# A gated attention-and-MLP decode kernel: the first weight load, 512 rows of wq, issued as two halves of 64 partitions from two engines

## The chip, the cores and the metric

The kernel runs on one core of one Trainium2 chip. The metric is the device time of one execution in microseconds; the time before is the median of three runs.

## The reference

One decode step for eight sequences: attention over a cached K and V, an MLP behind a layer norm, and a gate that mixes the two. Everything is bf16.

```python
# x: [8, 1, 576]; 32 heads of 128; 4096 cached keys; MLP width 4608
g = sigmoid((x * gate_w).sum(-1, keepdims=True))
q = (x @ wq) -> [8, 32, 1, 128]                    # wq: [576, 4096]
p = softmax(q . k_cache * 128 ** -0.5)             # k_cache: [8, 32, 4096, 128]
a = (p . v_cache) -> [8, 1, 4096] @ wo             # wo: [4096, 576]
b = gelu(layernorm(x) @ w1 + b1) @ w2 + b2         # w1: [576, 4608], w2: [4608, 576]
out = g * a + (1 - g) * b
```

The K and V caches are 268 MB each, the weights together about 20 MB. Each byte of them is read once.

## The kernel before

**Groups.** A group `n` (32 of them) is one sequence and eight heads. Its K is 8.4 MB, laid out in SBUF as 128 partitions with 256 keys each, and so is its V. The scores are made by VectorE: `mult` (L501) multiplies 32 keys of each partition with the group's query `q_n`, TensorE adds up pieces of the products (L512 and L183), and VectorE reduces the rest (L524). Eight such steps make the scores of a group. After the softmax TensorE multiplies with V (L565), while VectorE is on the next group's K.

**Buffers and order of the loads.** `KR` holds one and a half K groups, `VB` one V group. SyncE's queue carries nearly every transfer, in program order, with a wait ahead of some of them. K of group n+1 (`load_k`, L333) waits until VectorE has read the half of the buffer that it overwrites; V (`load_v`, L344) waits until TensorE has finished with the V before it.

**The start.** Before the first group the same buffers hold weights. SyncE issues, in this order: rows 0 to 511 of wq into `VB` (4 MB: 128 partitions of 32 KB, four rows each), the last 64 rows of wq (`halves`, 128 partitions of 4 KB), K of group 0 in two parts, w1 in two parts. The second of these waits for `c_yps`, the last of three ScalarE blanks that write zeros into PSUM banks. Then comes w2 (`load_w2`), which waits for the last Q matmul (`p_Q`), because it goes into `VB` too; then K of group 1, which waits for the last product of group 0; then V of group 0, a first part that waits for `p_Q`, and a second that waits for the MLP's last matmul (L654), which reads w2 out of that place.

ScalarE's queue carries the small loads: x (8 partitions), gate_w, b1, b2, all issued right behind the three blanks in ScalarE's program. Its other work at the start is the table loads, the blanks (L289), two constants from the identity, the square root and the sigmoid (L410, L411), and copies.

x is needed for the layer norm and the gate (VectorE, from L398; gate_w at L408), for the transposes of x and of its normed form on TensorE (L425), and so for Q (L452): 40 matmuls with wq as the moving operand. TensorE runs in program order: transposes of x, of the normed x, then Q. ScalarE copies Q out (L455), TensorE spreads it to the partitions (L466), ScalarE makes `q_n` of it (L476), and the first product of group 0 follows on VectorE.

`op(engine, fn, waits, dma)` records an instruction for an engine with what it waits for; `load` is the same for a DMA with a semaphore of its own, so that the DMAs all carry line L296. The order in which the operations are recorded is the program order of each engine.

Of the kernel before, what the change touches and what calls it, by code (L numbers as in the profile page):

```python
# [41 lines left out]
class Stream:  # L42
# [11 lines left out]
    def op(self, engine, fn, waits=(), dma=None, side=0):  # L54

        rec = [fn, [w for w in waits if w is not None], None, dma, (engine, side)]
        self.ops[engine].append(rec)
        if dma is not None:
            return ("dma", *dma)
        return ("op", engine, rec)  # L60
# [84 lines left out]
def bass_gated_mix__mha_block_cached__mixer_channel_mlp__decode_kernel(  # L145
# [18 lines left out]
    op = S.op  # L164
# [4 lines left out]
    def pstride(t):  # L169
        return t[tuple([slice(None)] * len(t.shape))].ap[0][0]  # L170

    def view(t, offset, shape):
        ap = []
        stride = 1
        for n in reversed(shape[1:]):
            ap.insert(0, [stride, n])
            stride *= n
        return bass.AP(tensor=t, offset=offset, ap=[[pstride(t), shape[0]]] + ap)
# [16 lines left out]
    wq_sb = view(VB, 0, [128, 4, SK])  # L195
    wq_t = view(VB, 4 * SK, [128, SK // 2])
# [86 lines left out]
    sV = nc.alloc_semaphore("sV")  # L283
    nK, nV = [0], [0]

    zeros = bass.AP(tensor=mA, offset=1, ap=[[pstride(mA), 128], [0, 512]])

    def blank(ps):
        return aside("scalar", lambda e: e.activation(out=ps[:, :], in_=zeros, func=ACT.Copy), [c_mA])  # L289
# [1 line left out]
    c_mA = op("gpsimd", lambda e: e.memset(mA[:], 0.0))  # L291
    c_ps = [blank(ps) for ps in tr_ps]
    c_yps = blank(y_ps)

    def load(engine, dst, src, name, waits=()):
        return op(engine, lambda e: e.dma_start(dst, src), waits, dma=(nc.alloc_semaphore(name), 16))  # L296


    x_flat = A_x.rearrange("b s d -> (b s) d")
    out_flat = out.rearrange("b s d -> (b s) d")  # L300
# [5 lines left out]
    def halves(w):  # L306

        return w[512:576, :].rearrange("r (s n) -> (r s) n", s=2)

    ld_wq = [load("sync", wq_sb, A_wq[0:512, :].rearrange("(p kt) n -> p kt n", kt=4), "ld_wqa"),  # L310
             load("sync", wq_t, halves(A_wq), "ld_wqb", [c_yps])]


    def kv_src(cache, n):
# [21 lines left out]
    def load_k_half(n, s):  # L336
        dst = view(KR, k_base(n) + s * THIRD, [128, NTK, DH])
        k_land[n, s] = load("sync", dst, kv_src(A_k_cache, n)[:, s * NTK:(s + 1) * NTK, :], f"sKh{n}_{s}")
# [561 lines left out]
```

## Time and profile before

| | |
|---|---|
| median of 3 runs | 1295.03 us (1294.98 to 1295.03) |
| span of the profiled execution | 1293.2 us |
| the profiled execution's own time | not given apart from the span |
| bytes moved, mean rate | 557.07 MB, 431 GB/s |
| busy: TensorE, VectorE, ScalarE, GpSimd | 57%, 66%, 6%, 1% |
| DMA engines, SyncE's queue / ScalarE's queue | 11520 packets, 556.93 MB / 200 packets, 0.03 MB |

The profile gives one execution: busy times by engine, 40 equal slices of the span, the DMA queues, the chain of work that ended last, groups of instructions by line, and the DMA issues. "SPq" and "ACTq" are the sequencers of SyncE and ScalarE, which issue DMAs; q1 is SyncE's DMA queue and q10 is ScalarE's. A timeline row has start, duration, engine, line, operation, the tiles written and read, how many instructions it merges, and in brackets the idle time ahead of it with what ended it.

### The profile page before, as it was taken

What the parts mean: (1) busy time and instruction counts of PE and PEld (TensorE: products, weight loads), DVE (VectorE), ACT (ScalarE), POOL (GpSimd) and SP (SyncE); (2) the same over time, 40 slices, a digit from 0 to 9 for tenths busy, and PEclk for the clock granted to TensorE, in tenths of its full rate; (3) what the DMA queues carried; (4) which work ended last, traced back from release to release, by engine and by line L of the source; (5) the groups of instructions that cost most, each with busy time, mean ns of one, the idle gap of its engine ahead of it and who ended that gap; (6) DMA issues with size and microseconds to landing.
All of it is one profiled execution on the core that took longest, in us unless ns stands there. A gap on an engine that the chain in (4) does not pass through costs nothing.

```text
span 1293.2 us, 10904 instructions
## 1 busy us (share of the span) xinstructions
PE 733.4 (57%) x4824; PEld 142.9 (11%) x3032; DVE 852.0 (66%) x1078; ACT 73.2 (6%) x164; POOL 12.7 (1%) x23
## 2 busy tenths in 40 slices
PE   3755566455556555556555556555556555557556
PEld 0211111011111011111011111001111001111003
DVE  3646667766667766667766667766668766667763
ACT  3300000000000000000000000000000000000001
POOL 0100000000000000000000000000000000000001
PEclk8978888877898787799778889777888877898888
DMA  9999999999999999999999999999999999999998
GB/s 406 426 447 424 430 442 428 434 436 432 442 426 430 444 426 430 442 430 434 436 430 442 426 430 444 426 430 442 430 434 436 430 442 428 428 444 428 432 434 356
DMA packets 11728, 557.07 MB, mean 431 GB/s; under 512 B 1448, under 2 KB 1608, under 8 KB 2120
## 3 DMA queue, kind: packets, MB, share of 16 engines
q1 hardware_dynamic: 11520, 556.93, 99.7%
q8 instruction: 5, 0.08, 0.0%
q10 hardware_dynamic: 200, 0.03, 0.0%
q14 instruction: 3, 0.02, 0.0%
HBM read 556.95 MB, written 0.01 MB: 431 GB/s over the span
## 4 chain that ended last, share of the span: by engine, by line
DMA 67%; DVE 18%; PE 9%; issue 5%; DVEq 1%; ACT 0%; SPq 0%; ACTq 0%
DMA KR<-in_A_k_cache_dram 65%; DVE p L501 15%; PE psb L183 7%; DVE s_sb L524 2%; DMA KR<-in_A_wo_dram 2%; PE psb L512 2%; DVEq L524 0%; DVEq L137 0%; SPq L296 0%; ACT psb L289 0%; PE psb L755 0%; ACT L289 0%; ACTq L296 0%; DVE p L851 0%; ACT sel_f L391 0%
## 5 line engine op out<-in xcount | busy, mean ns | idle before, releaser
L501 DVE TENSOR_TENSOR p<-KR,q_n 128x4096 bf16<-128x4096 bf16 x256 | 581.9, 2284 | 212.7 <-DMA KR<-in_A_k_cache_dram 212.7
L183 PE MATMUL psb<-p,ident 128*128 128x512 bf16 x1792 | 485.8, 416 | 0.0
L512 PE MATMUL psb<-p,ident 128*128 128x512 bf16 x256 | 112.3, 439 | 509.6 <-DVE p L501 509.6
L524 DVE TENSOR_REDUCE s_sb<-psb 128x512 f32 (+1 forms) x256 | 175.6, 686 | 107.5 <-PE psb L183 61.0
L512 PEld LDWEIGHTS psb<-p,ident 128*128 128x128 bf16 x256 | 26.1, 102 | 964.3 <-DVE p L501 963.9
L565 PE MATMUL psb<-VB,P 128*32 128x512 bf16 x1984 | 112.8, 380 | 0.0
L553 DVE TENSOR_SCALAR P<-E,own 128x256 bf16<-128x256 bf16 x256 | 53.1, 282 | 87.4 <-ACT E L550 87.4
L476 ACT ACTIVATE q_n<-q_bc 128x128 bf16<-128x128 bf16 x32 | 9.9, 310 | 871.4 <-DVE p L501 871.3
L565 PEld LDWEIGHTS psb<-VB,P 128*32 128x32 bf16 x1984 | 50.2, 97 | 47.8
L582 PE MATMUL psb<-selO,O_sb 128*128 128x8 f32 x256 | 33.9, 259 | 22.5 <-ACT O_sb L577 22.5
L582 PEld LDWEIGHTS psb<-selO,O_sb 128*128 128x128 f32 x256 | 31.0, 191 | 38.3 <-ACT O_sb L577 38.3
L577 ACT ACTIVATE O_sb<-psb 128x512 f32<-128x512 f32 x32 | 19.1, 597 | 197.9 <-PE psb L565 197.9
L572 PEld LDWEIGHTS psb<-rs,ones 128*128 128x128 f32 x64 | 12.1, 190 | 46.6 <-issue 44.4
L692 POOL TENSOR_TENSOR p<-OT_sb,fine 128x512 bf16<-128x512 bf16 (+1 forms) x4 | 5.0, 1276 | 1196.9 <-PE psb L572 1193.1
L550 ACT ACTIVATE E<-s_sb,mD 128x256 bf16<-128x256 f32 x32 | 16.0, 499 | 0.0
L541 DVE TENSOR_REDUCE mA<-s_sb 128x1 f32<-128x256 f32 x32 | 13.5, 420 | 1.1
L481 ACT ACTIVATE OT_sb<-O_n,G 128x8 bf16<-128x8 f32 x31 | 9.3, 301 | 84.3 <-DVE O_n L588 84.3
L556 DVE TENSOR_REDUCE es<-E 128x1 f32<-128x256 bf16 x32 | 13.2, 412 | 0.0
L572 PE MATMUL psb<-rs,ones 128*128 128x8 f32 x64 | 9.2, 216 | 1.3 <-DVE O_n L588 1.3
L654 PE MATMUL psb<-VB,hT_sb 128*8 128x288 bf16 x72 | 6.5, 357 | 4.7 <-POOL hT_sb L633 4.7
L557 DVE TENSOR_SCALAR rs<-own,es 128x8 f32<-128x8 f32 x32 | 7.4, 231 | 1.1
L549 DVE STREAM_TRANSPOSE mD<-mC 128x32 f32<-128x32 f32 x32 | 6.8, 212 | 1.1
(98 smaller groups left out, 125.6 us busy)
## 6 DMA issues: line engine op xcount, KB each, us to landing
KR<-in_A_k_cache_dram SPq DMA_DIRECT2D x2, 4096.0 KB, 24.8
VB<-in_A_v_cache_dram SPq DMA_DIRECT2D x1, 5376.0 KB, 27.1
VB<-in_B_w_dram SPq DMA_DIRECT2D x1, 5184.0 KB, 40.7
KR<-in_B_w_dram SPq DMA_DIRECT2D x1, 4608.0 KB, 41.2
VB<-in_A_wq_dram SPq DMA_DIRECT2D x1, 4096.0 KB, 12.5
KR<-in_A_v_cache_dram SPq DMA_DIRECT2D x1, 4096.0 KB, 22.3
VB<-in_A_v_cache_dram SPq DMA_DIRECT2D x1, 2816.0 KB, 38.4
KR<-in_A_wo_dram SPq DMA_DIRECT2D x1, 2304.0 KB, 20.7
```

The costliest lines, as they stand in the source:

```text
L183: return e.add_instruction(mybir.InstMatmult(name=nc.get_next_instruction_name(), engine=mybir.EngineType.PE, ins=[e.lower_ap(rhs), e.lowe ...
L501: v_mult[n, c] = op("vector", lambda e: e.tensor_tensor(out=p1[:, par, :, :], in0=k_of(), in1=qb, op=ALU.mult), [k_land[n, s], a_q[n], p_s ...
L512: fn = lambda e, r=r: e.matmul(tr_ps[par][:, :], lhsT=ident[:, :], rhs=r, start=True, stop=False)
L524: v_red[n, c] = op("vector", lambda e: e.tensor_reduce(out=s_of(), in_=tr_ps[par][:, :].rearrange("p (t c) -> p t c", c=CH), axis=AX.X, op ...
L541: t = op("vector", lambda e: e.tensor_reduce(out=mA[:, 0:1], in_=s_sb[:, :], axis=AX.X, op=ALU.max), [v_red[n, NC - 1], c_mA])
L550: a_exp[n] = op("scalar", lambda e: e.activation(out=E[:, :], in_=s_sb[:, :], func=ACT.Exp, bias=mD[:, 0:1], scale=1.0), [v_nm[n], v_P.get ...
L553: v_P[n] = op("vector", lambda e, h=h: e.tensor_scalar(out=P[:, :, h, :], in0=E[:, :].rearrange("p (q t) -> p q t", t=TQ), scalar1=own[:, ...
L556: t = op("vector", lambda e: e.tensor_reduce(out=es[:, :], in_=E[:, :], axis=AX.X, op=ALU.add), [a_exp[n]])
L565: p_pv[n] = op("tensor", lambda e, o=o, tq=tq, at=at, v=v: e.matmul(o, lhsT=P[:, tq, :, :].rearrange("p h t -> p (h t)"), rhs=v.rearrange( ...
L572: p_z[n] = op("tensor", lambda e: e.matmul(oz_ps[:, HB:2 * HB], lhsT=ones[:, :], rhs=rs[:, :], start=True, stop=True), [v_rs[n], v_norm.ge ...
L577: a_ev[n] = op("scalar", lambda e: e.activation(out=O_sb[:].rearrange("p t d -> p (t d)"), in_=o_ps[n // last][:, :], func=ACT.Copy), [p_p ...
L582: p_oz[n] = op("tensor", lambda e, tt=tt: e.matmul(o, lhsT=O_sb[:, tt, :], rhs=selO[:, tt, :], start=(tt == 0), stop=(tt == TQ - 1 and stop)),
```

## The change

The 4 MB load of wq's rows 0 to 511 becomes two loads of 2 MB: partitions 0 to 63 from SyncE, partitions 64 to 127 from ScalarE. Each has a semaphore of its own. Both are recorded ahead of everything else, so that ScalarE's half is the first instruction of its program, ahead of the blanks and the small loads. The first Q matmul waits for three loads of wq instead of two. The rest of the order stays.

```diff
+    def load(engine, dst, src, name, waits=()):
+        return op(engine, lambda e: e.dma_start(dst, src), waits, dma=(nc.alloc_semaphore(name), 16))
+
+    wq_src = A_wq[0:512, :].rearrange("(p kt) n -> p kt n", kt=4)
+    ld_wq = [load(e, wq_sb[p:p + 64], wq_src[p:p + 64], f"ld_wqa{p}") for e, p in (("sync", 0), ("scalar", 64))]
+
     zeros = bass.AP(tensor=mA, offset=1, ap=[[pstride(mA), 128], [0, 512]])
...
-    def load(engine, dst, src, name, waits=()):
-        return op(engine, lambda e: e.dma_start(dst, src), waits, dma=(nc.alloc_semaphore(name), 16))
-
-
...
-    ld_wq = [load("sync", wq_sb, A_wq[0:512, :].rearrange("(p kt) n -> p kt n", kt=4), "ld_wqa"),
-             load("sync", wq_t, halves(A_wq), "ld_wqb", [c_yps])]
+    ld_wq.append(load("sync", wq_t, halves(A_wq), "ld_wqb", [c_yps]))
```

## The prediction

> **What bounds the kernel now.** I read the page's head first: the span, the slices of DMA, the queues, the chain.
>
> ```profile
> span 1293.2 us, 10904 instructions
> ...
> DMA  9999999999999999999999999999999999999998
> ...
> q1 hardware_dynamic: 11520, 556.93, 99.7%
> ...
> DMA 67%; DVE 18%; PE 9%; issue 5%; DVEq 1%; ACT 0%; SPq 0%; ACTq 0%
> ```
>
> The 16 DMA engines are busy in all 40 slices, and SyncE's queue (q1) fills 99.7% of their time. The chain names DVE for 18%, but only because a K load's landing lets DVE free the buffer of the next one; the engines meanwhile work on V. The same by stages (columns after the engines: clock, DMA share, GB/s):
>
> ```profile
> 0.00:1.75 1.75, 0.00 (x0) 0.00 (x0) 0.18 (x1) 1.00 (x1) 0.98 (x9) 1.00 0.00 0
> 1.75:32.33 30.58, 11.16 (x70) 2.92 (x58) 10.76 (x20) 9.06 (x19) 0.96 (x5) 0.89 1.03 430
> 32.33:1265.83 1233.50, 703.70 (x4428) 128.01 (x2648) 833.37 (x1035) 59.62 (x138) 4.97 (x6) 0.84 1.00 433
> 1265.83:1293.20 27.37, 18.52 (x329) 12.02 (x327) 7.65 (x24) 3.47 (x7) 5.80 (x5) 0.77 0.84 349
> ```
>
> Nothing moves for 1.75 us, then the stream runs at 430 to 433 GB/s until the tail. So the time is start plus bytes over rate plus tail, and a microsecond lost or won in the first transfer reaches the end whole, unless the stream has a hole elsewhere. The median, 1295.03 us, lies 1.8 us above this execution's span; that is launch and finish outside it, which the change does not touch. The profiled execution's own time outside the trace is not shown, so I add to the median.
>
> Now the first transfer in the trace by queue (one line for each window and queue: packets, MB, share of 16 engines). Windows in order: 1.50 to 2.75, 2.75 to 3.50 (totals); 3.25 to 4.60, 4.60 to 5.75 (q10, ScalarE's); 7.00 to 8.25 (q1); 11.00 to 11.75 (both); 11.75 to 12.25 (total).
>
> ```profile
> DMA packets 15, 0.49 MB, mean 393 GB/s; under 512 B 0, under 2 KB 0, under 8 KB 0
> DMA packets 1, 0.03 MB, mean 44 GB/s; under 512 B 0, under 2 KB 0, under 8 KB 0
> q10 hardware_dynamic: 8, 0.01, 1.8%
> q10 hardware_dynamic: 8, 0.00, 0.4%
> q1 hardware_dynamic: 16, 0.52, 97.0%
> q1 hardware_dynamic: 16, 0.52, 161.9%
> q10 hardware_dynamic: 16, 0.00, 1.6%
> DMA packets 0, 0.00 MB, mean 0 GB/s; under 512 B 0, under 2 KB 0, under 8 KB 0
> ```
>
> A packet is entered where it starts. wq goes as 128 packets of 32 KB in eight rounds of 16, one for each engine, a round every 1.25 us (7.00 to 8.25: 97% of 16 engines, so 1.21 us a packet, 27.0 GB/s an engine). Three things are to be seen. ScalarE's packets start only where SyncE's start (11.00 to 11.75, then none for half a microsecond): an engine takes the two queues in turn, by whole packets. x, 8 partitions, goes as 8 packets in one round and 8 more of almost no bytes in the next (I take them for its completion writes): each partition had an engine of its own, so a transfer is spread by its count of partitions. And the engines run nearly in step: a round's starts lie within 0.75 us, the first one's mostly within 1.0 us (15 of 16 by 2.75).
>
> **The change part by part.**
>
> ```profile
> 0.75 3.28 SPq L296 DMA_DIRECT2D VB<-in_A_wq_dram  x2
> 0.75 1.28 ACT L289 ACT_TABLE_LOAD   x1 [0.75 <-PEq L885]
> 0.91 0.58 ACTq L296 DMA_DIRECT2D p<-in_A_x_dram  x1
> 2.58 1.10 ACT L289 ACTIVATE psb<-mA 128x512 f32<-128x512 f32 x2
> 4.08 0.96 SPq L296 DMA_DIRECT2D KR<-in_A_k_cache_dram  x2
> 5.75 0.74 DVE L398 TENSOR_REDUCE stat<-p 8x1 f32<-8x576 bf16 x1 [3.02 <-DMA p<-in_A_x_dram]
> 8.29 0.75 DVE L408 CUSTOM_DVE_ANT_0 p<-p 8x576 bf16<-8x576 bf16 x1 [0.52 <-DMA p<-in_gate_w_dram]
> 11.56 0.35 PE L425 MATMUL psb<-ident,p 8*128 8x8 bf16 x6 [1.27 <-ACT p L418]
> 14.73 4.42 PE L452 MATMUL psb<-VB,p 128*8 128x512 bf16 x40 [2.81 <-DMA VB<-in_A_wq_dram]
> 19.18 0.33 SPq L296 DMA_DIRECT2D VB<-in_B_w_dram  x1
> 20.91 0.31 ACT L476 ACTIVATE q_n<-q_bc 128x128 bf16<-128x128 bf16 x1
> 24.31 4.49 DVE L501 TENSOR_TENSOR p<-KR,q_n 128x4096 bf16<-128x4096 bf16 x2 [12.15 <-DMA KR<-in_A_k_cache_dram]
> 47.21 0.33 SPq L333 DMA_DIRECT2D KR<-in_A_k_cache_dram  x1
> 65.07 6.47 PE L654 MATMUL psb<-VB,hT_sb 128*8 128x288 bf16 x72 [4.69 <-POOL hT_sb L633]
> 79.59 4.49 DVE L501 TENSOR_TENSOR p<-KR,q_n 128x4096 bf16<-128x4096 bf16 x2 [19.79 <-DMA KR<-in_A_k_cache_dram]
> ```
>
> SyncE keeps its count of DMAs, the first with half the rows; ScalarE gets one more, ahead of all it has. By parts:
>
> ScalarE. The new issue takes at most what its first one takes, 0.58 us. The table load and the three blanks, the last ending at 3.68, and the issues of x, gate_w, b1 and b2 move back by that. SyncE waits for the last blank before it issues the last 64 rows of wq, and K0 and w1 stand behind that in program order: the K issue goes from 4.08 to about 4.7. Cost nothing: the engines hold the two halves until past 12 us. Without that cover it would cost 0.6 us.
>
> Completion writes: 16 more, one an engine, of 12 ns (1.6% of 16 engines for 0.75 us, over 16): 0.01 us. TensorE's first Q matmul waits for one semaphore more; it has idle time there.
>
> x moves most. In ScalarE's queue it now stands behind four 32 KB packets an engine, which alternate with SyncE's four. Eight turns of 1.25 us end by 13.0; then a completion turn, x's turn and its completion, short ones: DVE has x at about 14.0, not 5.75. From x to the end of the transposes are 6.2 us (5.75 to 11.91), so Q starts at 20.2 rather than 14.73 (+5.4). w2, which waits for Q, is issued at 24.6, not 19.18. q_n comes 5.4 us later, at 26.6, so the first product starts 2.3 us after K0's landing, and K1's issue, which waits for its last product, goes from 47.21 to 49.5. What covers all this is w2, which stands in the queue at that moment:
>
> ```profile
> VB<-in_B_w_dram SPq DMA_DIRECT2D x1, 5184.0 KB, 40.7
> VB<-in_A_wq_dram SPq DMA_DIRECT2D x1, 4096.0 KB, 12.5
> ```
>
> Issued at 19.18, w2 lands 40.7 us later, at 59.9 (the row below it is wq's, from 0.75 to 13.25); K1's issue may be 12 us late, less some 2 for the way from issue to first packet, before the stream has a hole. The second part of V0 waits for the 72 matmuls that end at 71.5; K1 lands only just before 79.6, so that too has 8 us. Cost nothing, but each microsecond beyond 10 would cost one.
>
> The start. A queue has 64 first packets to make instead of 128, and two queues make them. First packets began from 1.75 to about 2.75; halving that spread is worth up to 0.5 us, and all that can be won is the 1.0 us from issue to first packet. A loss: 0.2 if two queues hinder each other. I take -0.2, near zero, because the 0.75 us spread of the later rounds absorbs most of it.
>
> The halves themselves carry the sum. Spread by count, 64 partitions are four for each of 16 engines, no longer eight; I infer that from x's row. Then in a turn of SyncE's queue all engines write partitions 0 to 63, in a turn of ScalarE's 64 to 127. Whether half of SBUF's partitions take 431 GB/s no row shows: all large transfers here have 128. The bounds: at the low end a packet costs 1.25 us as now, +0. At the high end half the partitions take half the rate, two engines share what one had, and a packet costs 2.5 us: 8 x 1.25 = +10.0 us. Two engines that share and are d apart run alone for d in each packet, so it takes 2.5 - d. Starts of 16 engines over 1.0 us, halved with the descriptors, make d some 0.3: 8 x 0.95 = +7.6 us; d = 1.0 would make it 2.0.
>
> Which end? Two rows lean to the high one (21 to 37 us, then 600 to 640):
>
> ```profile
> DMA packets 236, 6.88 MB, mean 430 GB/s; under 512 B 32, under 2 KB 32, under 8 KB 32
> DMA packets 298, 17.11 MB, mean 428 GB/s; under 512 B 37, under 2 KB 37, under 8 KB 37
> ```
>
> Packets of 29 KB in the mean and of 57 KB, from different tensors, run at one rate. So it is not the source nor the packet's size that sets it; what stays the same is the 16 engines and the 128 partitions they write. Either can be the ceiling, and only the second makes this change dear. I take the second by a narrow margin: turns by whole packets and engines in step are just the case in which nothing evens it out.
>
> [...]
>
> Sum: +7.6 - 0.2 = +7.4, on 1295.03: 1302.4 us, 0.57% slower. The stream stays behind by that to the end, since it has no idle slice in which to catch up: x then lands at 21.6, the first product starts at 34.3 and K1 is issued at 57.2, while w2 lands at 67.5, so the cover holds.
>
> **The rivals.** (1) The halves run at full rate, the engines being the ceiling: 8 turns of 1.25 us as now, x late but covered. 1294.8 us, no change (1294.3 to 1295.3). For it: 27.0 GB/s an engine looks the same for any transfer; against it: nothing but the lean above. This is the case on the other side, and it decides as soon as half the partitions take the full 431 GB/s.
>
> (2) Engines fall out of step, because the queues' first packets reach some of them in the other order (half on SyncE's packet, half on ScalarE's): then both halves of SBUF are written at once and most of the loss goes, +0.5 to +5: about 1298. Against it: SyncE issues first and rounds stay in step through all eight in the trace.
>
> (3) The late x opens a hole: K1's issue more than 10 us late relative to the stream. It needs x 8 us later than I have it; each microsecond beyond costs one. Two such on top of the main case would give 1304.
>
> (4) Faster by more than 0.2%, 2.6 us: one mechanism only, the start; the stream would have to begin before the kernel does, as just 1.75 us lie ahead of the first packet. If all of it went: 1293.3, still within 0.2%.
>
> (5) The change does not do what it says: both halves one after the other in effect. That is the high end of the main case, 1305.
>
> **How the numbers follow.** 0.2%, 2.6 us, is about what a measurement of this kernel can tell from no change. The main case (+6 to +10) has 0.44, (2) 0.10, of which 0.07 above 2.6 us, (3) and (5) 0.04; (1) 0.39; (4) 0.03. That makes slower 0.55, same 0.42, faster 0.03. The likeliest case's own range is 1301 to 1305. As (1) can't be left out of a range that holds 8 in 10, it runs from 1294.6 to 1304.9.
>
> **What would show it.** In the changed profile: q1 and q10 both with 32 KB packets at the start; packets there at about 2.2 us instead of 1.2, the first windows near 240 GB/s instead of 420; wq landing near 20, not 13; x at DVE near 21; K0's first product at about 34; K1's landing near 87 instead of 79.5, and every later K by the same 7 to 8 us, at the same 433 GB/s. Packets of 1.21 us and K1 landing near 79 would show (1): then the step that is wrong is the ceiling of half the partitions. K1's landing later than the first K's shift would show (3). First packets before 1.6 us would show a larger gain at the start.

## The result and the profile after

The changed kernel takes 1304.91 us (1304.83 to 1304.93, five runs), the kernel before 1295.03 us. The ratio is 1.0076 (95% interval 1.0065 to 1.0086): 9.9 us slower. The forecast was 1302.4 us, slower, with a range up to 1304.9; the time lies on its upper edge.

The head of the page of the changed kernel, and its span by stages (us, engines, clock, DMA share, GB/s):

```profile
span 1303.0 us, 10905 instructions
...
GB/s 275 434 427 433 441 429 441 429 441 427 441 427 443 424 437 433 427 441 427 441 429 441 429 441 427 441 427 443 424 435 435 427 441 429 439 429 441 429 429 362
...
q1 hardware_dynamic: 11456, 554.84, 98.9%
q10 hardware_dynamic: 280, 2.13, 0.8%
```

```profile
1.75:22.00 20.25, 0.00 (x0) 0.00 (x0) 0.68 (x3) 4.56 (x7) 0.67 (x4) 1.00 0.97 213
22.00:42.00 20.00, 8.89 (x62) 2.73 (x55) 7.97 (x15) 4.52 (x11) 0.31 (x1) 0.86 1.04 436
42.00:1275.00 1233.00, 710.35 (x4433) 128.12 (x2649) 835.48 (x1036) 60.25 (x139) 4.99 (x6) 0.84 1.00 433
```

The loss is one slice: 275 GB/s in the first of 40 against 406 before, the others about as before. For 20 us, while the two halves are under way, the engines are as busy as ever (0.97) and move 213 GB/s, just half of 430. From then on it is 433 as before. The rounds of packets, the windows 8.50 to 10.25, 10.25 to 11.25 and 11.25 to 12.50:

```profile
q1 hardware_dynamic: 16, 0.52, 135.2%
DMA packets 0, 0.00 MB, mean 0 GB/s; under 512 B 0, under 2 KB 0, under 8 KB 0
q10 hardware_dynamic: 16, 0.52, 189.7%
```

All sixteen engines start on a packet of SyncE's queue (partitions 0 to 63), then all on one of ScalarE's (64 to 127). In these two rounds a packet takes 2.37 us (135.2% of 16 engines for 1.75 us, over 16 packets; 189.7% for 1.25 us gives the same) instead of 1.21. The eight rounds come from SyncE, SyncE, ScalarE, SyncE, ScalarE, SyncE, ScalarE, ScalarE.

The timeline of the changed kernel, the rows that answer to those of before (lines moved by one), and below it w2 in the list of DMA issues:

```profile
23.52 0.74 DVE L399 TENSOR_REDUCE stat<-p 8x1 f32<-8x576 bf16 x1 [20.78 <-DMA p<-in_A_x_dram]
34.20 0.33 SPq L287 DMA_DIRECT2D VB<-in_B_w_dram  x1
36.33 4.49 DVE L502 TENSOR_TENSOR p<-KR,q_n 128x4096 bf16<-128x4096 bf16 x2 [6.42 <-ACT q_n L477]
59.23 0.33 SPq L334 DMA_DIRECT2D KR<-in_A_k_cache_dram  x1
89.38 4.49 DVE L502 TENSOR_TENSOR p<-KR,q_n 128x4096 bf16<-128x4096 bf16 x2 [17.56 <-DMA KR<-in_A_k_cache_dram]
```

```profile
VB<-in_B_w_dram SPq DMA_DIRECT2D x1, 5184.0 KB, 35.6
```

x is 17.8 us late, and the first product waits for `q_n`, no longer for K0. Still, K1 is issued at 59.23 while w2 holds the engines until 69.8 (34.20 + 35.6). K1 is there 9.8 us later than before (89.38 against 79.59), and 9.8 us is what the span has grown by.

### The profile page after: what moved, and what is told of

The parts are those of the page before. It is cut to its first block, busy times and chain, and to the rows that moved or that the text cites. A ratio compares the mean times of both kernels' runs of the same rounds, so it can differ in the third digit from the quotient of the medians.

```text
span 1303.0 us, 10905 instructions
## 1 busy us (share of the span) xinstructions
PE 739.3 (57%) x4824; PEld 143.9 (11%) x3032; DVE 851.7 (65%) x1078; ACT 73.2 (6%) x164; POOL 12.7 (1%) x23
## 4 chain that ended last, share of the span: by engine, by line
DMA 66%; DVE 18%; PE 9%; issue 4%; DVEq 1%; ACT 0%; SPq 0%; ACTq 0%; POOL 0%
DMA KR<-in_A_k_cache_dram 63%; DVE p L502 16%; PE psb L183 7%; DVE s_sb L525 2%; DMA KR<-in_A_wo_dram 2%; DMA p<-in_A_x_dram 2%; PE psb L513 1%; DVEq L525 0%; DVEq L137 0%; PE psb L453 0%; SPq L287 0%; PE psb L756 0%; DVE stat L399 0%; PE psb L426 0%; DVE p L400 0%
## 6 DMA issues: line engine op xcount, KB each, us to landing
VB<-in_B_w_dram SPq DMA_DIRECT2D x1, 5184.0 KB, 35.6
```

## The experiments

Each is an edit of the changed kernel; all but the pads' extra load leave the work as it is. `wq_src` is wq with four rows a partition.

**Same two queues, whole partitions.**

```diff
-    ld_wq = [load(e, wq_sb[p:p + 64], wq_src[p:p + 64], f"ld_wqa{p}") for e, p in (("sync", 0), ("scalar", 64))]
+    ld_wq = [load(e, wq_sb[:, k:k + 2], wq_src[:, k:k + 2], f"ld_wqa{k}") for e, k in (("sync", 0), ("scalar", 2))]
```

> The two queues stay, SyncE and ScalarE each issue 2 MB as their first DMA, but each load now covers all 128 partitions and half of the columns (16 KB a partition instead of 32). Theory H (half of the partitions takes half the rate): packets run at 27 GB/s again, 0.61 us each, the first stretch at 420 GB/s or more, wq is in by 13.5 us and the time is 1295.0 us (1294.5 to 1295.6), although x still stands behind ScalarE's part and reaches VectorE at about 14. Rival Q (two queues issuing and alternating at the start hinder each other, whatever they write): the stretch stays near 213 GB/s and the time at 1304 to 1305. Rival X (the late x is what costs): between, 1297 or more.

Measured: 1295.11 us (1294.99 to 1295.49), ratio to before 1.0001 (0.9992 to 1.0011). The first stretch, and x's arrival:

```profile
1.75:13.00 11.25, 0.00 (x0) 0.00 (x0) 0.67 (x3) 4.39 (x7) 0.66 (x4) 1.00 0.99 397
13.36 0.74 DVE L399 TENSOR_REDUCE stat<-p 8x1 f32<-8x576 bf16 x1 [10.63 <-DMA p<-in_A_x_dram]
27.20 4.49 DVE L502 TENSOR_TENSOR p<-KR,q_n 128x4096 bf16<-128x4096 bf16 x2 [7.44 <-ACT q_n L477]
```

Two queues, the same bytes on each, ScalarE's half first in its program, x late by 7.6 us and the first product waiting for `q_n`: everything of the change but the division by partitions, and the loss is gone. That refutes the rival of the two queues. It shows that an x late by 7.6 us costs nothing; the 17.8 us of the changed kernel are tested below. It also shows that nothing is won at the start.

**Same halves, one queue.**

```diff
-    ld_wq = [load(e, wq_sb[p:p + 64], wq_src[p:p + 64], f"ld_wqa{p}") for e, p in (("sync", 0), ("scalar", 64))]
+    ld_wq = [load(e, wq_sb[p:p + 64], wq_src[p:p + 64], f"ld_wqa{p}") for e, p in (("sync", 0), ("sync", 64))]
```

> Both halves of 64 partitions are issued by SyncE, one behind the other; ScalarE's queue is as in the kernel before, so x is not late. Theory H: each half runs alone on half of the partitions, 8 packets an engine of 2.37 us instead of 1.21, +9.3 us: 1304.3 us (1303.8 to 1304.8), x at VectorE somewhat after 6 us since its turns are longer. Rival Q: no second large queue, so 1295.0. Rival X: 1295 to 1296.

Measured: 1305.47 us (1305.35 to 1305.64), with 209 GB/s over the 20 us in which the changed kernel had 213:

```profile
1.75:22.00 20.25, 0.66 (x12) 0.52 (x12) 4.14 (x16) 6.37 (x14) 0.97 (x5) 1.00 1.00 209
```

The loss needs no second queue. It is 10.4 us, a microsecond above what I expected. The expectation took 2.37 us a packet from the changed kernel, where the halves alternate. Here the rounds of one half follow one another, and a packet takes 2.57 us (the round at 6.25 to 8.00: 146.6% of 16 engines for 1.75 us, over 16):

```profile
q1 hardware_dynamic: 16, 0.52, 146.6%
```

**x first.** x and gate_w are recorded ahead of ScalarE's half.

```diff
+    ld_x = load("scalar", x_sb, x_flat, "ld_x")
+    ld_gw = load("scalar", gw8, bcast(gate_w), "ld_gw")
     ld_wq = [load(e, wq_sb[p:p + 64], wq_src[p:p + 64], f"ld_wqa{p}") for e, p in (("sync", 0), ("scalar", 64))]
...
-    ld_x = load("scalar", x_sb, x_flat, "ld_x")
-    ld_gw = load("scalar", gw8, bcast(gate_w), "ld_gw")
```

> The changed kernel with x and gate_w issued ahead of ScalarE's half of wq, so x is at VectorE by about 6 to 9 us instead of 23.5; the halves stay on their two queues. Theory H: the late x costs nothing (w2 covers it), so the time stays at 1304.9 us (1304.3 to 1305.2). Rival X: the part of the 9.9 us that belongs to the late x comes back; all of it would be 1295.

Measured: 1305.58 us (1305.36 to 1305.73), with VectorE on x already at 2.65 us:

```profile
2.65 0.73 DVE L399 TENSOR_REDUCE stat<-p 8x1 f32<-8x576 bf16 x1
```

Nothing comes back: x early by 21 us changes nothing for the better, so its lateness cost nothing. The time lies 0.4 us above the expected range. Behind x, ScalarE's half starts later, and SyncE's first three rounds run one after the other: the third takes 2.56 us a packet (6.75 to 7.75) where the changed kernel's third, from ScalarE, took 2.35 (188.2% of 16 engines for 6.50 to 7.75).

```profile
q1 hardware_dynamic: 16, 0.52, 255.9%
```

That goes the way of the 0.7 us by which this kernel is slower than the changed one; no run isolates it.

**Which 64 partitions.** All from SyncE: partitions 32 to 95, then 0 to 31, then 96 to 127.

```diff
-    ld_wq = [load(e, wq_sb[p:p + 64], wq_src[p:p + 64], f"ld_wqa{p}") for e, p in (("sync", 0), ("scalar", 64))]
+    ld_wq = [load("sync", wq_sb[p:q], wq_src[p:q], f"ld_wqa{p}") for p, q in ((32, 96), (0, 32), (96, 128))]
```

> SyncE issues three loads: partitions 32 to 95, then 0 to 31, then 96 to 127. The first has 64 partitions too, but half of them from each half. If the ceiling belongs to a set of entries that partitions 0 to 63 share and 64 to 127 do not (Hp), the first load runs at full rate (four packets an engine of 1.21 us) and the two outer ones at half (two each of 2.4 us): +4.6 us, 1299.7 us (1299.2 to 1300.2). If the ceiling goes by the count of partitions (Hc), the first runs at half rate and the outer ones at a quarter: 4 x 1.16 + 4 x 3.6 = +19 us, 1314 us. If 64 partitions in one load were the trouble by themselves, the first would be slow and the rest unknown.

Measured: 1300.63 us (1300.49 to 1300.97), +5.6, which is 0.4 above the range of Hp and far from Hc. The windows of the middle load and of the two outer ones, by stages, then a round of each (3.75 to 4.75 and 14.25 to 15.50):

```profile
3.75:7.50 3.75, 0.00 (x0) 0.00 (x0) 1.10 (x7) 3.44 (x5) 0.00 (x0) 1.00 0.99 422
7.50:17.00 9.50, 0.66 (x12) 0.52 (x12) 1.35 (x6) 0.93 (x5) 0.31 (x1) 1.00 1.02 222
```

```profile
q1 hardware_dynamic: 16, 0.52, 123.2%
q1 hardware_dynamic: 16, 0.52, 203.8%
```

These rows bear most on what the ceiling is. The middle load has 64 partitions like each half, on as many engines with as many packets, and runs at 422 GB/s, 1.23 us a packet. The outer loads have 32 partitions each and run at the rate of a half, 222 GB/s and 2.55 us a packet, not at a quarter. So it is neither the count of partitions nor the size of the load; what sets the load at 422 apart is that it reaches 32 partitions of each half, and the others one half alone. One rival is left, the source: in all these runs a row of wq goes to the same partition, so another half of the partitions is also another stretch of wq. A short stretch is not slow as such. The last 64 rows of wq, half a megabyte in one piece, go to all 128 partitions, and in the kernel before they come at 413 GB/s (12.75 to 13.25):

```profile
DMA packets 84, 0.21 MB, mean 413 GB/s; under 512 B 34, under 2 KB 34, under 8 KB 84
```

No run sends the same rows to other partitions.

**Out of step by an extra load.** An unused load of 28 KB into each of partitions 0 to 7 goes ahead, then the halves in either order, or wq whole as a control. All are on SyncE.

```diff
-    ld_wq = [load(e, wq_sb[p:p + 64], wq_src[p:p + 64], f"ld_wqa{p}") for e, p in (("sync", 0), ("scalar", 64))]
+    pad = view(VB, 4 * SK + SK // 2, [128, 112 * DH])
+    ld_wq = [load("sync", pad[0:8], A_k_cache[0, 0, 0:896].rearrange("(p r) d -> p (r d)", p=8), "ld_pad")]
+    ld_wq += [load("sync", wq_sb[p:p + 64], wq_src[p:p + 64], f"ld_wqa{p}") for p in (64, 0)]     # or (0, 64)
+    # control, in place of the line above: ld_wq += [load("sync", wq_sb, wq_src, "ld_wqa")]
```

> All on SyncE: first an extra load (pad) of 28 KB into each of partitions 0 to 7, whose data nobody uses, which by x's row goes to eight engines, one packet each; then partitions 64 to 127 of wq, then 0 to 63. Theory P (two engines, one of the first eight and one of the last eight, share one way into SBUF, and the loss comes only while both are on the same half): the pad's eight packets crowd into two such ways and take about 4.2 us, four packets' time; after it the first eight engines write the high half while the last eight write the low half, then the low half while the last eight are on the next loads in the high partitions. All packets of wq run at 1.2 us, and the only loss is the pad's: 1299.3 us (1298.5 to 1300.3), the same as the control with a whole wq. Theory H without pairs (a load of 64 contiguous partitions always runs at half rate): packets of 2.4 us, 1305.5 plus 0.6 to 4: 1306 to 1310.

> The same loads with the two halves in the other order: pad, partitions 0 to 63, then 64 to 127. Theory P: the first eight engines write the low half while the last eight write the high one (1.2 us a packet), but then they write the high half while the last eight, ahead by the pad, write the next loads into the same high partitions: four packets of 2.4 us, +4.9 us on the other order, 1304 us (1302.5 to 1305.5). Theory H without pairs: no difference from the other order, 1306 to 1310.

> Control: the pad, then wq's 512 rows in one load of 128 partitions, as in the kernel before, all on SyncE. Theory P: the pad holds eight engines for about 4.2 us and everything behind it is that late: 1299.3 us. If the pad's packets do not crowd (1.1 us each), 1296.1 us, and the two kernels with halves then have to be read against this.

Measured: 1307.86 us (1307.79 to 1308.17) for high then low, 1309.39 us (1309.27 to 1309.48) for low then high, 1298.28 us (1297.83 to 1298.48) for the control. Theory P is wrong: beyond the control, the halves cost 9.6 and 11.1 us, about as much as without a pad. The control came out between the two values expected for it. Theory H had expected no difference between the two orders; what makes the 1.5 us was not traced. From high then low, the windows 12.25 to 13.40, 13.60 to 14.00 and 14.00 to 14.70:

```profile
q1 hardware_dynamic: 8, 0.26, 108.0%
q1 hardware_dynamic: 16, 0.26, 310.5%
DMA packets 0, 0.00 MB, mean 0 GB/s; under 512 B 0, under 2 KB 0, under 8 KB 0
```

The pad did put two groups of eight engines out of step, but by half a packet only. At 12.25 to 13.40 one group starts its last high packets (eight); from 13.60 the other starts low ones (eight, and eight completions). Until past 14.70, so for at least 0.7 us of each low packet, eight engines write the high half and eight the low one, and still the eight low packets take 2.48 us each (310.5% of 16 engines for 0.40 us, over 8). So a pair of engines that shares one way in, one from each group, is not the picture. Whether engines share anything, and which, no run shows. The pad itself, 0.23 MB, costs the control 3.25 us, against the 0.5 us that so many bytes take at 431 GB/s: packets into eight neighbouring partitions are slow as well, 2.8 us for 28 KB (last section).

**Shorter turns.** The halves on their two queues again, cut by columns, so that a packet is a run of 4 KB or of 1 KB; as a control, runs of 1 KB from both queues over all partitions.

```diff
-    ld_wq = [load(e, wq_sb[p:p + 64], wq_src[p:p + 64], f"ld_wqa{p}") for e, p in (("sync", 0), ("scalar", 64))]
+    ld_wq = [load(e, wq_sb[p:p + 64, :, c:c + 2048], wq_src[p:p + 64, :, c:c + 2048], f"ld_wqa{p}_{c}")
+             for c in range(0, SK, 2048) for e, p in (("sync", 0), ("scalar", 64))]        # 1 KB: 512 for 2048
+    # control: wq_sb[:, :, c:c + 512] from wq_src[:, :, c:c + 512], SyncE and ScalarE in turn
```

> The changed kernel's two halves on their two queues, but each in two loads of half the columns, so that a packet is a run of 4 KB instead of 32 KB and an engine changes from one half of the partitions to the other every 0.15 us of full-rate time, far less than the 0.75 to 1.25 us by which the engines' starts are spread. Theory T (the loss is made by long turns: all engines on one half for a whole 32 KB packet): the engines are now mixed over both halves, most of the loss goes, 1295 to 1298 us. Theory N (loads of 64 contiguous partitions are slow however the two are mixed): first stretch near 213 GB/s, 1304 to 1306 us.

> As before with eight loads a half of 512 columns each, runs of 1 KB, turns of 0.04 us. Theory T: 1295 to 1298 us plus whatever runs of 1 KB cost by themselves (the control with whole loads shows that). Theory N: 1304 to 1306 plus the same.

> Control: the same runs of 1 KB from the two queues in turn, but each load covers all 128 partitions (eight loads of 512 columns). Both theories: only the price of short runs and of the issues, 1295 to 1297 us.

Measured: 1302.05 us (1301.55 to 1302.47) with 4 KB, 1299.67 us (1299.42 to 1300.05) with 1 KB. The control's nine executions fell on two levels, four at 1298.3 to 1298.4 and five at 1305.2 to 1306.2; only one of the lower level has a trace, and what makes the upper one is open. So the totals don't say what short runs cost by themselves; the traces do. Three stretches with 4 KB, then 9 to 15 us with 1 KB in halves, then the same in the control:

```profile
3.00:5.00 2.00, 0.00 (x0) 0.00 (x0) 0.00 (x0) 1.99 (x5) 0.00 (x0) 1.00 0.94 223
9.00:13.00 4.00, 0.00 (x0) 0.00 (x0) 0.00 (x0) 0.00 (x0) 0.00 (x0) 1.00 1.02 325
15.00:17.00 2.00, 0.00 (x0) 0.00 (x0) 0.74 (x2) 0.00 (x0) 0.00 (x0) 1.00 1.07 203
```

```profile
9.00:15.00 6.00, 0.00 (x0) 0.00 (x0) 0.00 (x0) 2.11 (x4) 0.00 (x0) 1.00 1.10 344
```

```profile
9.00:15.00 6.00, 0.00 (x0) 0.00 (x0) 0.00 (x0) 0.00 (x0) 0.00 (x0) 1.00 1.11 346
```

From 3 to 5 us only ScalarE's queue runs (109 packets, all of q10), so one half of the partitions: 223 GB/s. From 9 to 13 both run in turn: 325 (no run has whole loads in runs of 4 KB beside it). From 15 on ScalarE's half is done (its queue moves 0.01 MB of 0.41): 203. In turns of 1 KB the halves run at 344, as fast as whole loads with the same runs, 346. So a half alone has run at 203 to 223 GB/s here, and two halves under way together ran faster than that in short turns, at 325 with 4 KB and 344 with 1 KB. Turns of 32 KB, the changed kernel, ran at 213 and cost 9.9 us, against 10.4 for one half behind the other. Runs of 1 KB have a price of their own: even the control's lower level is 3.3 us above the kernel before, and above the 1295 to 1297 expected. Of the expectation for short turns the rate of the mixed halves held (344 beside 346) and the size did not: the 4 KB kernel was to come to 1295 to 1298 us, and its stretches with one queue alone, which I had not counted, keep it at 1302.

No version here beats the kernel before: its whole load in one DMA already runs at the stream's rate, 1.21 us a packet (7.00 to 8.25), and 16 engines at 27.0 GB/s make 432.

## Why the prediction was right, and where its steps were off

**The stream as the bound.** Right: the first stretch's loss reached the end undiminished (K1's products 9.8 us late, the span 9.8 us longer), at the same 433 GB/s afterwards.

**Half of the partitions takes half of the rate.** Right for these loads: the middle load ran at 422 GB/s beside outer loads at 222, with the stretch of wq as the one rival left. The ground on which I leaned to it, one rate for all packet sizes, did not prove it; rival (1), the engines as the ceiling, was not excluded by any row of before. With 0.44 for the main case and 0.39 for that rival the choice was near a toss, and that it fell on the right side is partly luck. The experiment excludes the rival: the same 16 engines ran at both rates.

**The size of it.** Here the sum was off: 8 x 0.95 = 7.6 us, with a packet that takes twice as long less d = 0.3 us of staggering, in each of eight rounds. The rounds were not alike. The first took 2.06 us a packet against 1.9 before, so it lost little. The second (3.75 to 5.25) and the last (18.00 to 19.75) took 2.55 and 2.54, the five between them 2.35 to 2.38, against 1.21:

```profile
q1 hardware_dynamic: 16, 0.52, 170.1%
q10 hardware_dynamic: 16, 0.52, 145.3%
```

The long rounds are those that follow a round on the same half; the short ones follow a round on the other half. In the kernel with the halves on one queue it is the same: 2.54 to 2.57 after the first round, but 2.43 where the half changes (11.50 to 13.10: 151.9% of 16 engines for 1.60 us, over 16 long packets). So a packet came out shorter by some 0.2 us only at a change of half: the term d was too large and stood in too many rounds. That two engines share what one had, on which d rests, was my assumption, and no run shows it. That staggered engines make the difference fits these rows and is not isolated; where the pad had put eight engines about a microsecond behind the other eight, packets took 2.48 us all the same. Added up, the rounds lost about 8.6 us, and they began 0.3 us later; the high end, +10.0, was nearly reached. The halves' last packets end by about 22.0, wq's ended by about 12.8 before (the last starts are at 19.5 and 11.5). That is 9.2 of the 9.8 us.

**The rest, about 0.6 us.** I had nothing for it. It lies in the last 64 rows of wq, 128 packets of 4 KB behind the halves. The same rows of both kernels (12.25 to 14.00 before, 20.75 to 23.75 after; q1, then q10):

```profile
q1 hardware_dynamic: 170, 0.95, 130.5%
q10 hardware_dynamic: 88, 0.01, 3.8%
```

```profile
q1 hardware_dynamic: 156, 0.98, 98.6%
q10 hardware_dynamic: 140, 0.03, 6.8%
```

SyncE's packets hold each engine for 2.96 us (98.6% of 3.00) where about as much data took 2.28 (130.5% of 1.75). ScalarE's small packets hold it for 0.20 instead of 0.07 us. That more small packets stand beside is not the cause: in the kernel with whole partitions on two queues 154 of them come beside the same data in 1.75 us (12.25 to 14.00), and it loses nothing.

```profile
q1 hardware_dynamic: 169, 0.98, 135.8%
q10 hardware_dynamic: 154, 0.03, 8.6%
```

The 4 KB packets themselves take longer. Before (12.75 to 13.25) it is 0.16 us each; in the changed kernel, while the last of ScalarE's long packets still run (21.00 to 22.00), it is 0.31 (50.2% of 16 engines for 1.00 us, over 26):

```profile
q1 hardware_dynamic: 51, 0.20, 100.5%
q1 hardware_dynamic: 26, 0.11, 50.2%
```

So the load behind the halves is slowed as well, a cost for which the sum had no term.

**The start, -0.2.** Wrong in sign: q1's first packets started at 2.1 instead of 1.8, their round ran until 3.15 rather than 2.75, and whole loads from two queues, which start at 1.8, won nothing (1295.11 us). That the spread of the first starts halves with a queue's packets, on which this part and d rest, was my estimate, and no run shows it. What makes the halves start later was not traced.

**x late, but covered.** Right. x came at 23.5 us (21.6 forecast), the first product at 36.3 (34.3), K1's issue at 59.2 (57.2), with w2 until 69.8 (67.5). All is two microseconds later, for the size above, and x first made nothing faster.

**Rival (2), engines out of step.** The order of queues did not break the step. Where a pad did, by half a packet, packets stayed at 2.48 us. What evened out the halves was short turns (344 GB/s with 1 KB), not an offset of half a long one.

## What to carry to other kernels

Let a large load into SBUF reach into both halves of the partitions at once: here large loads into 128 partitions ran at 430 to 433 GB/s (at 346 in runs of 1 KB) and one into 32 to 95 at 422, while loads into one half alone ran at 203 to 223. Divide a large load by columns if it has to go over two queues; with runs of 16 KB a partition that cost nothing here (1295.11 us against 1295.03). In this kernel, which a DMA stream bounds, the 9.8 us by which K1 came late were still lost at the end, while a compute chain with x 17.8 us late cost nothing: a large transfer, w2, stood in the queue until 69.8 us, and K1, which waits for the chain, was issued at 59.2.

## What the runs showed of the hardware that was not expected

A load into 8 neighbouring partitions, 0.23 MB, cost a stream of 431 GB/s 3.25 us. In its shadow the other eight engines' first packets took about 3.6 us (the control, windows 1.50 to 2.00 and 2.00 to 3.00):

```profile
q1 hardware_dynamic: 8, 0.23, 282.9%
q1 hardware_dynamic: 8, 0.26, 181.0%
```

The pad's eight packets of 28 KB take 2.8 us each (282.9% of 16 engines for 0.50 us, over 8), the other eight 3.6 us (181.0% for 1.00 us), against about 1.9 us for the first packets of the kernel before (145.8% of 16 engines for 1.25 us, 15 packets). They were not kept up by the pad's own partitions: in the kernel with the pad and the high half first they write partitions 64 to 127, and take 3.5 us too (177.4% for the same 1.00 us). By what path the pad slows them no run here shows.
